# A spectral filter and a low-rank mixer: batch 2's first stage two slots later, and pairs of batches 1 to 3 in other slots

## The chip, the cores and the metric

The kernel runs on one core of a Trainium2 chip. The metric is the time of one execution on the device in microseconds (us). It is taken from runs without a profile; beside them one execution was profiled, and all durations, waits and clocks in this document come from such a profile.

The engines are TensorE (PE in the profile; PEld is its weight load), VectorE (DVE), ScalarE (ACT), GpSimd (POOL) and SyncE (SP). SyncE, ScalarE and GpSimd also issue DMAs. Each engine goes through its own list of instructions in order.

## The reference

```python
def _attn_ref(x, filt_r, filt_i):              # x: 8 x 3136 x 256
    X = np.fft.rfft(x, axis=1)
    Y = X * (filt_r + 1j * filt_i)[None, :, :]
    return np.fft.irfft(Y, n=x.shape[1], axis=1)

def _moe_ref(x, U, V, w_ch1, w_ch2):           # U: 3136 x 32, V: 32 x 3136, w_ch1: 256 x 1024
    h = x.transpose(0, 2, 1) @ U @ V
    u = x + h.transpose(0, 2, 1)
    return u + np.maximum(u @ w_ch1, 0.0) @ w_ch2
```

The second function takes the result of the first. All inputs and the output are float32.

## The kernel before

The Fourier transform of 3136 = 64 x 49 points is done as matmuls in two stages, and so is its inverse. For each batch from 1 to 7 the way is:

- `load_x` (L154) brings one of three chunks of x into a tile `xt`, as float16, by DMAs of GpSimd. There are five such buffers.
- `f1_units` (L451) is the first stage, 13 units for a batch: one matmul (L460) into a PSUM bank `pf` and one eviction into `asb` (L464 on VectorE or L466 on ScalarE). Units 0 to 3 belong to chunk 0, 4 to 7 to chunk 1, 8 to 12 to chunk 2. After a chunk's last unit `asb` is stored into the DRAM scratch `c1` (L470): by SyncE for batch 1, by GpSimd for the others.
- `load_a` (L477) reads `c1` back, rearranged, as one of four tiles `a` of a batch, by SyncE (L480). Each serves four pairs, and there are three buffers.
- `stream` (L526) does the second stage, the filter and the first inverse stage, for 16 pairs of frequencies per batch. A pair is two matmuls into `px` (L499, a single bank) and the product with the filter (for batch 1 `both_products`, L507, one instruction of VectorE; for the others `product`, L518 and L520, three of VectorE, and a sum on GpSimd, L523). The inverse of a pair (`i1`, matmuls L535 into `pi`, eviction L539) is issued `LAG` = 2 pairs later; each fourth one is followed by a store into the scratch `c2` (L542).
- `load_e` (L483) reads `c2` back as the tiles `e2`; `h1_unit` (L563) computes the low-rank part from them.
- The mixer then goes over groups of four row blocks, six groups to a batch: `make_u` (L659), `mm1` (L689, matmuls L694 into `phh`, relu into `h` at L702 or L700) and `mm2` (L704, matmuls L720 or L765 into `po`), with the output behind them.

Batch 0 has a way of its own (`first_f1`, `first_mid`) ahead of the main loop, in which batch 1's first stage begins too. The main loop runs over the mixer's groups of all batches, and everything else of the batches ahead is woven into it by slots: `put(slot, generator)` enters one step in a table, and `run(slot)` issues the steps of a slot in the order in which they were entered. A group has eight slots, a batch `SB` = 48:

```python
        for a in range(4):
            if live:
                mm1(gx, 2 * a)
                mm1(gx, 2 * a + 1)
            if full:
                run(slot)
            ...                       # a == 2: make_u of the next group
            mm2(gx - 1, a)
            if full:
                run(slot + 1)
                slot += 2
            evict(gx - 1, a)
```

The list `steps` holds the slots of the pairs, one entry for each `next` of `stream`. Since this order is written out by hand, an engine's instructions stand in the order of the slots, and a step that must wait holds up all that stands behind it on its engine.

Of the kernel before, what the change touches and what calls it, by code (L numbers as in the profile page):

```python
# [15 lines left out]
NS = 32  # L16
# [5 lines left out]
KG = 8  # L22
LAG = 2
# [66 lines left out]
def kernel(  # L90
# [12 lines left out]
    nb = x.shape[0]  # L103
# [19 lines left out]
    def bank(tag, name):  # L123
        return ps.tile([128, 512], F32, tag=tag, bufs=BUFS[tag], name=name)
# [14 lines left out]
    def natural(ap):  # L139

        return ap.rearrange("p (r i h a) -> p r h i a", i=4, h=2, a=32)

    def split(ap):

        return ap.rearrange("p (r h i a) -> p r h i a", i=4, h=2, a=32)
# [305 lines left out]
    def f1_units(b, both):  # L451
        ne = 0
        for c in range(len(CH)):
            xt = st[b]["x"].pop(c)
            asb = sb.tile([128, 9 * DM], F16, tag="asb", bufs=2, name="asb")
            for n0 in range(0, CH[c], 2):
                w = min(2, CH[c] - n0) * DM
                k = 64 if c0[c] + n0 == NH - 1 else 128
                pf = bank("o" if b == 1 else "m", "pf")
                nc.tensor.matmul(pf[:, 0:w], w64[:, :], xt[:, n0 * DM:n0 * DM + w],  # L460
                                 start=True, stop=True)
                dst = asb[0:k, n0 * DM:n0 * DM + w]
                if both and (ne % 2 if b > 1 else ne > 3 and ne not in (5, 7, 12)):
                    nc.vector.tensor_copy(dst, pf[0:k, 0:w])  # L464
                else:
                    nc.scalar.copy(dst, pf[0:k, 0:w])  # L466
                ne += 1
                if n0 + 2 >= CH[c]:
                    for h, o, n in span(c0[c], c0[c + 1]):
                        (nc.sync if b == 1 else nc.gpsimd).dma_start(c1[b].ap()[:, o:o + n], asb[64 * h:64 * h + 64, 0:n])  # L470
                yield


    def spec(t, gi, p, n):
        return bass.AP(tensor=t, offset=gi * KG * 2 * RD + p * DM, ap=[[DM, n], [2 * RD, KG], [1, DM]])
# [18 lines left out]
    def forward(m, a2, xtags):  # L494
        ml = m % (KG // 2)
        px = bank(xtags[m % len(xtags)], "px")
        for sl in range(2):
            s = 2 * m + sl
            nc.tensor.matmul(px[:, sl * DM:(sl + 1) * DM], t2[:, s * 128:(s + 1) * 128],  # L499
                             a2[:, (2 * ml + sl) * DM:(2 * ml + sl + 1) * DM],  # L500
                             start=True, stop=True, skip_group_check=True)
        return px
# [23 lines left out]
    def stream():  # L526
        pend = []

        def i1(b, m, y, esb):
            pi = bank("f", "pi")  # L530
            nf = 2 if b == 1 else 1
            for sl in range(2):
                for fi in range(nf):
                    g, o = (fi * NS + 2 * m + sl) * 98, fi * 512 + sl * DM
                    nc.tensor.matmul(pi[0:98, sl * DM:(sl + 1) * DM], g12[:, g:g + 98],  # L535
                                     y[:, o:o + DM], start=(fi == 0), stop=(fi == nf - 1),
                                     skip_group_check=True)
            gi, ml = divmod(m, KG // 2)
            nc.scalar.copy(split(esb[:, ml * 512:(ml + 1) * 512]), natural(pi[0:98, :]))  # L539
            if ml == KG // 2 - 1:  # L540
                for p, n in ((0, 96), (96, 2)):
                    (nc.scalar if b == 1 else nc.sync).dma_start(  # L542
                        spec(c2[b], gi, p, n), esb[p:p + n].rearrange("p (k d) -> p k d", d=DM))

        for b in range(1, nb):
            for m in range(NS // 2):
                gi, ml = divmod(m, KG // 2)
                if ml == 0:
                    esb = sb.tile([98, KG * DM], F16, tag="esb", bufs=2, name="esb")
                y = (both_products if b == 1 else product)(m, forward(m, st[b]["a"][gi], ("x",)))  # L550
                if len(pend) == LAG:
                    i1(*pend.pop(0))
                pend.append((b, m, y, esb))
                yield
        for p in pend:
            i1(*p)
            yield

    def one(load, *a):
        load(*a)  # L560
        yield
# [227 lines left out]
    def put(slot, gen):  # L789
        sched.setdefault(int(slot + 0.5), []).append(gen)  # L790
# [6 lines left out]
    NP = NS // 2  # L797
    GP = NP // (NS // KG)
    SB = 48
# [13 lines left out]
    fill = f1_units(1, True)  # L813
# [8 lines left out]
    for k in range(2):  # L822
        put(k, fill)

    steps = [8.8 + 1.25 * k for k in range(NP)] + [28 + 2.45 * k for k in range(NP)]
    for b in range(3, nb):
        steps += [SB * (b - 2) + 18 + 3 * k for k in range(NP)]
    steps += [steps[-1] + 3 * (k + 1) for k in range(LAG)]
    mid = stream()
    for b in range(1, nb):  # L830
        gen = h1_unit(b)
        for t in (8, 7, 6) if b > 1 else (9, 8, 7):
            put(SB * b - t, gen)
    for k, t in enumerate(steps):
        put(t, mid)
        b, m = divmod(k - LAG, NP)
        if k >= LAG and m % GP == GP - 1:
            t += 6 if b > 1 or not b and m < NP - 1 else 4
            late = SB * b + 13
            if b and t < late:  # L840
                put(max(t, SB * b - 1), one(load_e, b + 1, m // GP, (0,)))
                put(late, one(load_e, b + 1, m // GP, (1,)))
            else:
                put(t, one(load_e, b + 1, m // GP))
    for b in range(1, nb):
        for gi in range(NS // KG):
            t = steps[NP * (b - 1) + GP * gi]
            put(max(2, t - (14 if b > 3 else 9 + b // 3)), one(load_a, b, gi))
        if b > 1:
            fill = f1_units(b, b == 2)  # L850
            t0 = steps[NP * (b - 1)]
            for k in range(NF):
                put(4 + 1.1 * k if b == 2 else 18 + 2.8 * k if b == 3 else t0 - 54 + 3 * k, fill)
            for c in range(len(CH)):
                if b > 2 or c > 0:
                    put(6 * c - 5 if b == 2 else 9 + 8 * c if b == 3 else t0 - 72 + 12 * c, one(load_x, b, c))
# [58 lines left out]
```

## Time and profile before

| what | value |
|---|---|
| runs | 533.61, 534.28, 538.67 us; median 534.28 us |
| the profiled execution's own time | 534.16 us |
| its span, first to last instruction | 532.4 us |
| mean granted TensorE clock | 0.988 of full |
| TensorE busy | 498.4 us (94% of the span) |
| VectorE, ScalarE, GpSimd busy | 400.7, 377.7, 290.9 us |
| TensorE idle from 0 to 54.5 us, 54.5 to 160 us, 160 to 500 us | 17.5, 7.2, 3.9 us |

The span is what the rows of the profile cover; the execution's time is 1.8 us longer. The first 54.5 us are batch 0's own way; the main loop's slot 0 is at 54.5 us and slot 66 at 158 us. Waits on engines other than TensorE matter only if TensorE comes to wait for them. A DMA has no busy time on the engine that issues it: its row tells when it was issued. Queue q0 in the DMA counts holds the transfers that GpSimd issues, q1 those of SyncE, q10 those of ScalarE.

### The profile page before, as it was taken

Reading aid. Unit: us, or ns where it says so; the run is one execution under the profiler, and the core shown is the slowest. Engines: PE = TensorE matmul, PEld = TensorE weight load, DVE = VectorE, ACT = ScalarE, POOL = GpSimd, SP = SyncE. Lnnn points to the kernel's source line nnn. Section 1 sums busy time; section 2 is a strip of 40 time slices with the busy share of each in tenths; the row PEclk is TensorE's granted clock in tenths of the full one; section 3 lists DMA queues with packets and bytes.
Section 4 is the critical chain, followed back from the end, with each engine's and each line's share of the span. In section 5 each row is a group of like instructions: output and inputs, shape, how many; then the busy total and the mean of one; then the engine's idle time right before and its main releaser. Section 6 shows DMA issues by size and latency. Waiting matters only on the chain.

```text
span 532.4 us, 11368 instructions
## 1 busy us (share of the span) xinstructions
PE 498.4 (94%) x4022; PEld 303.0 (57%) x4022; DVE 400.7 (75%) x574; ACT 377.7 (71%) x771; POOL 290.9 (55%) x412
## 2 busy tenths in 40 slices
PE   3877799999999999999999999989999999999995
PEld 3765266667667785555555555545555555454444
DVE  7897367757786758898998888978999877445663
ACT  2767756677678868888788878877777678765541
POOL 7797633345656456586677665765756564313000
PEclk9979989999999999999999999999999999999999
DMA  8989998986988577897989798896887575544324
GB/s 127 193 150 188 204 211 210 217 223 147 232 234 214 141 154 221 208 229 171 225 204 220 195 240 205 177 235 145 199 194 148 126 180 128 140 96 80 78 66 104
DMA packets 118426, 93.98 MB, mean 177 GB/s; under 512 B 52977, under 2 KB 100786, under 8 KB 118370
## 3 DMA queue, kind: packets, MB, share of 16 engines
q0 software_dynamic: 21936, 41.91, 38.3%
q1 hardware_dynamic: 93226, 49.75, 37.7%
q10 hardware_dynamic: 3208, 1.61, 1.1%
q8 instruction: 31, 0.51, 0.4%
q14 instruction: 25, 0.20, 0.1%
HBM read 56.25 MB, written 48.17 MB: 196 GB/s over the span
## 4 chain that ended last, share of the span: by engine, by line
PE 79%; DVE 6%; POOL 6%; DMA 6%; issue 2%; ACT 1%; DVEq 0%; POOLq 0%; ACTq 0%
PE phh L694 27%; PE po L765 21%; PE po L720 8%; PE px L499 5%; PE pi L535 5%; PE pu L620 4%; DVE uv L520 3%; PE pf L460 3%; DMA xt<-in_x_dram 3%; PE ph L577 2%; POOL low L284 2%; DVE uv L518 1%; DMA vq<-in_moe_V_dram 1%; DMA g<-gd 1%; POOL xt L154 1%
## 5 line engine op out<-in xcount | busy, mean ns | idle before, releaser
L702 ACT ACTIVATE h<-phh 128x512 f16<-128x512 f32 (+1 forms) x391 | 205.9, 578 | 71.8 <-PE phh L694 66.9
L694 PE MATMUL phh<-ut,w 128*128 128x512 f16 x768 | 197.6, 379 | 0.6 <-ACT h L702 0.3
L523 POOL TENSOR_TENSOR y<-uv 128x512 f16<-128x512 f16 x96 | 111.0, 1158 | 110.6 <-DVE uv L520 74.8
L765 PE MATMUL po<-h,w 128*128 128x512 f16 x560 | 143.8, 379 | 0.0
L520 DVE TENSOR_TENSOR uv<-px,ft 64x512 f16<-64x512 f32 x192 | 132.1, 688 | 2.6
L694 PEld LDWEIGHTS <-w 128*128 128x128 f16 x832 | 78.5, 98 | 77.2 <-issue 2.4
L518 DVE TENSOR_TENSOR uv<-px,ft 128x512 f16<-128x512 f32 x96 | 65.3, 680 | 42.1 <-PE px L499 35.8
L783 POOL DMA_DIRECT2D out_dram<-och x120 | 70.2, 592 | 42.9 <-DVE och L775 35.6
L539 ACT CAST esb<-pi 98x512 f16<-98x512 f32 x112 | 66.0, 589 | 36.9 <-PE pi L535 33.9
L765 PEld LDWEIGHTS <-w 128*128 128x128 f16 x560 | 51.6, 98 | 53.2 <-issue 1.1
L774 DVE TENSOR_TENSOR tt<-po,ut 128x512 f32<-128x512 f32 x70 | 48.4, 692 | 33.8 <-PE po L765 30.9
L720 PE MATMUL po<-w,h 128*128 128x256 f16 x448 | 58.9, 275 | 0.0
L499 PE MATMUL px<-a,t 98*128 98x256 f16 x256 | 50.0, 277 | 7.2 <-DVE uv L520 3.7
L775 DVE STREAM_TRANSPOSE och<-tt 128x512 f32<-128x512 f32 x70 | 49.8, 711 | 2.4
L466 ACT CAST asb<-pf 128x512 f16<-128x512 f32 (+1 forms) x79 | 45.7, 578 | 5.3 <-PE pf L460 4.2
L720 PEld LDWEIGHTS <-h 128*128 128x128 f16 x448 | 42.8, 98 | 10.8 <-issue 1.4
L507 DVE TENSOR_TENSOR uv<-px,ft 128x1024 f16<-128x1024 f32 x32 | 38.0, 1219 | 13.9 <-PE px L499 13.4
L499 PEld LDWEIGHTS <-t 98*128 98x128 f16 x256 | 23.0, 99 | 33.9 <-DVE uv L520 11.5
L535 PE MATMUL pi<-y,g 128*98 128x256 f16 x192 | 36.7, 271 | 2.0 <-POOL y L523 2.0
L684 ACT CAST ut<-pu 128x512 f16<-128x512 f32 x70 | 38.1, 610 | 0.0
L460 PE MATMUL pf<-xt,w 128*128 128x512 f16 (+1 forms) x91 | 33.4, 373 | 3.3 <-DMA xt<-in_x_dram 3.0
L535 PEld LDWEIGHTS <-g 128*98 128x98 f16 x256 | 29.6, 123 | 4.0 <-issue 2.1
(96 smaller groups left out, 445.0 us busy)
## 6 DMA issues: line engine op xcount, KB each, us to landing
xt<-in_x_dram POOLq DMA_DIRECT2D x46, 256.0 KB, 6.7
a<-c SPq DMA_DIRECT2D x28, 384.0 KB
e<-c SPq DMA_DIRECT2D x56, 192.0 KB
out_dram<-och SPq DMA_DIRECT2D x160, 64.0 KB
c<-esb SPq DMA_DIRECT2D x24, 384.0 KB
c<-asb POOLq DMA_DIRECT2D x30, 256.0 KB, 4.9
out_dram<-och POOLq DMA_DIRECT2D x120, 64.0 KB, 3.2
out_dram<-och POOLq DMA_DIRECT2D x24, 256.0 KB, 4.9
```

Of the source, the lines that this page charges most:

```text
L499: nc.tensor.matmul(px[:, sl * DM:(sl + 1) * DM], t2[:, s * 128:(s + 1) * 128], a2[:, (2 * ml + sl) * DM:(2 * ml + sl + 1) * DM], start=Tru ...
L518: nc.vector.tensor_mul(uv[:, 0:512], px[:, :], ft[:, a:a + 512])
L520: nc.vector.tensor_mul(uv[p:p + 64, 512:1024], px[q:q + 64, :], ft[q:q + 64, b:b + 512])
L523: nc.gpsimd.tensor_add(y, uv[:, 0:512], uv[:, 512:1024])
L535: nc.tensor.matmul(pi[0:98, sl * DM:(sl + 1) * DM], g12[:, g:g + 98], y[:, o:o + DM], start=(fi == 0), stop=(fi == nf - 1), skip_group_che ...
L539: nc.scalar.copy(split(esb[:, ml * 512:(ml + 1) * 512]), natural(pi[0:98, :]))
L694: nc.tensor.matmul(pm[:, 0:w], w1[:, dh * 1024 + t * 128:dh * 1024 + (t + 1) * 128], ut[:, dh * w:(dh + 1) * w], start=(dh == 0), stop=(dh ...
L702: nc.scalar.activation(h[:, 0:w], pm[:, 0:w], RELU)
L720: nc.tensor.matmul(po[:, o:o + DM], hs[gx, t][:, rr * 128:(rr + 1) * 128], w2[:, t * DM:(t + 1) * DM], start=(t == 0), stop=False, skip_gr ...
L765: nc.tensor.matmul(po[:, :], w2[:, t * DM + dh * 128:t * DM + (dh + 1) * 128], hs[gx, t][:, :], start=(t == 0), stop=(t == 7))
L775: nc.vector.transpose(och.rearrange("p (j h a) -> p h j a", h=2, a=32)[:, dh], tt.rearrange("p (j t) -> p j t", t=32))
L783: (nc.gpsimd if k and b < nb - 1 else nc.sync).dma_start(dst, och[32 * i:32 * i + 32, k * 512:(k + 1) * 512] .rearrange("p (r e) -> p r e" ...
```

## The change

- Batch 2's 13 first-stage units go from slots 4 + 1.1k to 6 + 1.2k (rounded: 4 to 17 before, 6 to 20 after). The loads of x keep their slots: batch 2's chunks 1 and 2 in slots 1 and 7, batch 3's chunks 0, 1 and 2 in slots 9, 17 and 25.
- Batch 1's last two inverses were issued with batch 2's first two pairs (slots 28 and 30); they get steps of their own (slots 29 and 30). Batch 7's last two had such steps already, and keep them.
- Batch 2's pairs go from 28 + 2.45k to 30 + 2.35k (last one in slot 65 in both), batch 3's from 66 + 3k to 67.5 + 2.9k (last one in slot 111 in both). Batch 1's pairs and those of batches 4 to 7 keep their slots.
- `load_a` and `load_e` follow their pairs by the new helper `pair(b, m)`: batch 2's four `load_a` go from slots 19, 29, 39, 48 to 22, 31, 41, 50, batch 3's first two from 56 and 68 to 58 and 69. `load_e` calls are entered after the pairs, so that within a slot they come after a pair and its inverse and no longer before.

```diff
@@ stream
-        for p in pend:
-            i1(*p)
-            yield
+            while pend and b in (1, nb - 1):
+                i1(*pend.pop(0))
+                yield
@@
-    steps = [8.8 + 1.25 * k for k in range(NP)] + [28 + 2.45 * k for k in range(NP)]
-    for b in range(3, nb):
+    steps = [8.8 + 1.25 * k for k in range(NP + LAG)] + [30 + 2.35 * k for k in range(NP)]
+    steps += [SB + 19.5 + 2.9 * k for k in range(NP)]
+    for b in range(4, nb):
         steps += [SB * (b - 2) + 18 + 3 * k for k in range(NP)]
@@
-    for k, t in enumerate(steps):
+    for t in steps:
         put(t, mid)
-        b, m = divmod(k - LAG, NP)
-        if k >= LAG and m % GP == GP - 1:
-            t += 6 if b > 1 or not b and m < NP - 1 else 4
-            late = SB * b + 13
-            ...
+
+    def pair(b, m):
+        return NP * (b - 1) + m + (LAG if b > 1 else 0)
+
     for b in range(1, nb):
         for gi in range(NS // KG):
-            t = steps[NP * (b - 1) + GP * gi]
-            put(max(2, t - (14 if b > 3 else 9 + b // 3)), one(load_a, b, gi))
+            t = steps[pair(b, GP * gi + GP - 1) + LAG]
+            t += 6 if b > 2 or b == 1 and gi < 3 else 4
+            late = SB * (b - 1) + 13
+            if b > 1 and t < late:
+                put(max(t, SB * (b - 1) - 1), one(load_e, b, gi, (0,)))
+                put(late, one(load_e, b, gi, (1,)))
+            else:
+                put(t, one(load_e, b, gi))
+    for b in range(1, nb):
+        for gi in range(NS // KG):
+            t = steps[pair(b, GP * gi)]
+            put(max(2, t - (14 if b > 3 else (9, 8, 10)[b - 1])), one(load_a, b, gi))
         if b > 1:
             fill = f1_units(b, b == 2)
-            t0 = steps[NP * (b - 1)]
+            t0 = steps[pair(b, 0)]
             for k in range(NF):
-                put(4 + 1.1 * k if b == 2 else 18 + 2.8 * k if b == 3 else t0 - 54 + 3 * k, fill)
+                put(6 + 1.2 * k if b == 2 else 18 + 2.8 * k if b == 3 else t0 - 54 + 3 * k, fill)
             for c in range(len(CH)):
                 if b > 2 or c > 0:
                     put(6 * c - 5 if b == 2 else 9 + 8 * c if b == 3 else t0 - 72 + 12 * c, one(load_x, b, c))
```

More of the change, by code (lines that the diff above doesn't have):

```diff
@@ L833 @@
             put(SB * b - t, gen)
-    for k, t in enumerate(steps):
+    for t in steps:
         put(t, mid)
-        b, m = divmod(k - LAG, NP)
-        if k >= LAG and m % GP == GP - 1:
-            t += 6 if b > 1 or not b and m < NP - 1 else 4
-            late = SB * b + 13
[L840 to L844, printed above, removed]
+    def pair(b, m):
+        return NP * (b - 1) + m + (LAG if b > 1 else 0)
     for b in range(1, nb):
         for gi in range(NS // KG):
-            t = steps[NP * (b - 1) + GP * gi]
-            put(max(2, t - (14 if b > 3 else 9 + b // 3)), one(load_a, b, gi))
+            t = steps[pair(b, GP * gi + GP - 1) + LAG]
[10 more added lines that the diff above has]
+            put(max(2, t - (14 if b > 3 else (9, 8, 10)[b - 1])), one(load_a, b, gi))
         if b > 1:
             fill = f1_units(b, b == 2)
-            t0 = steps[NP * (b - 1)]
+            t0 = steps[pair(b, 0)]
             for k in range(NF):
-                put(4 + 1.1 * k if b == 2 else 18 + 2.8 * k if b == 3 else t0 - 54 + 3 * k, fill)
+                put(6 + 1.2 * k if b == 2 else 18 + 2.8 * k if b == 3 else t0 - 54 + 3 * k, fill)
             for c in range(len(CH)):
```

## The prediction

> **What bounds the kernel now.** I read the page first, then TensorE's waits, the timelines around the slots that the change touches, and the DMA counts of a few stretches.
>
> ```profile
> PE 498.4 (94%) x4022; PEld 303.0 (57%) x4022; DVE 400.7 (75%) x574; ACT 377.7 (71%) x771; POOL 290.9 (55%) x412
> ```
>
> TensorE is busy for 498.4 of 532.4 us. Of its 34 idle us 17.5 lie before the main loop starts at 54.5 us, 7.2 between there and 160 us, where the changed slots are, and 3.9 from 160 to 500. So in the loop a wait of TensorE that goes, or comes, moves the end by about its own length. Its waits that lie in the changed slots, from its timeline (start, length, then the idle time before it and who ended that):
>
> ```profile
> 59.53 0.38 PE L460 MATMUL pf<-xt,w 128*128 128x512 f16 x1 [1.15 <-DMA xt<-in_x_dram]
> 66.15 0.58 PE L460 MATMUL pf<-xt,w 128*128 128x512 f16 x1 [1.85 <-DMA xt<-in_x_dram]
> 66.53 1.91 PE L720 MATMUL po<-w,h 128*128 128x256 f16 x8
> 68.45 0.63 PE L499 MATMUL px<-a,t 98*128 98x256 f16 x2
> 70.83 1.03 PE L720 MATMUL po<-w,h 128*128 128x256 f16 x8
> 104.00 0.38 PE L499 MATMUL px<-a,t 98*128 98x256 f16 x2 [0.99 <-DVE uv L507]
> 145.84 0.39 PE L499 MATMUL px<-a,t 98*128 98x256 f16 x2 [0.55 <-DVE uv L520]
> 158.11 0.39 PE L499 MATMUL px<-a,t 98*128 98x256 f16 x2 [1.18 <-DVE uv L520]
> ```
>
> The first two are first-stage units 0 and 4 of batch 2 (slots 4 and 8), waiting for x. 68.45 is batch 1's first pair (slot 9): it did not wait. 104.00 is batch 2's first pair, in one slot with batch 1's last; 158.11 is batch 3's first, one slot behind batch 2's last. The eight po matmuls took 1.91 us at 66.53 and 1.03 at 70.83: the clock. The windows (length, PE busy with instruction count, then the other engines, PEclk, DMA share, GB/s) say so:
>
> ```profile
> 62.49:65.90 3.41, 1.51 (x8) 0.48 (x5) 0.69 (x1) 2.38 (x6) 1.66 (x3) 1.00 0.98 203
> 65.90:69.32 3.42, 3.17 (x15) 1.98 (x16) 0.20 (x1) 0.59 (x1) 3.34 (x8) 0.50 1.20 217
> 69.32:72.73 3.41, 3.03 (x23) 2.13 (x22) 2.94 (x4) 1.08 (x2) 0.33 (x1) 1.00 1.10 286
> ```
>
> In this trace the granted clock changes only at edges 3.41 us apart: a stretch with 1.51 us of work is followed by one at 0.50, and a full one restores 1.00.
>
> **What the slots do to the queues.** GpSimd's and SyncE's own rows:
>
> ```profile
> 58.12 1.18 POOL L154 DMA_DIRECT2D xt<-in_x_dram x2
> 64.24 1.09 POOL L470 DMA_DIRECT2D c<-asb  x2 [4.94 <-ACT ul L296]
> 65.31 1.24 POOL L154 DMA_DIRECT2D xt<-in_x_dram  x2
> 67.91 1.17 POOL L154 DMA_DIRECT2D xt<-in_x_dram  x2
> ...
> 61.83 4.95 SPq L480 DMA_DIRECT2D a<-c  x6
> ```
>
> GpSimd issues x chunk 1 of batch 2 at 58.12, then stands for 4.94 us at the store of batch 2's first stage (unit 3, slot 7), and only behind it come x chunk 2 (65.31, slot 7) and batch 3's chunk 0 (67.91, slot 9). Unit 3 moves to slot 10, but these two loads stay in slots 7 and 9. So they pass the store: both buffers are free (batch 1's units ended at 56.15, the copies out of vq before 56.2), and GpSimd issues them at about 59.3 to 61.4 and, after one copy of 0.55, 62.0 to 63.1. That is the loss that I expect: SyncE issues batch 1's a tiles at 61.83, as soon as its c1 stores have landed (trace: 61.55), and these move beside the x loads. Packets by queue, in four stretches (66 to 69, 64 to 66, 149.5 to 151.5, 62 to 64 us, in this order):
>
> ```profile
> q1 hardware_dynamic: 1277, 0.64, 118.4%
> ...
> q1 hardware_dynamic: 751, 0.38, 73.9%
> q0 software_dynamic: 57, 0.09, 26.5%
> ...
> q0 software_dynamic: 213, 0.59, 94.8%
> q1 hardware_dynamic: 102, 0.05, 9.5%
> ...
> q0 software_dynamic: 162, 0.29, 91.0%
> ```
>
> Alone, the a loads on q1 move 1277 packets of 512 B in 3 us, 426 per us. Beside a full q0 (149.5 to 151.5, the end of a later a tile) they get 51 per us, fewer than q0's 107. I read this as taking turns packet by packet, with packets of q0 four times the size.
>
> **The sum, part by part.**
>
> 1. Units 0 and 4 no longer wait for x. TensorE comes to slot 9 at 68.45 less 3.00 of waits, less two units that now lie behind it (two pf, some 0.22 apart: 0.43) and less about 0.8 of half clock: 64.2 us.
>
> 2. There it waits for the a tile, which landed at 67.89 in the trace. After: from 64.0 q0 still holds 57 packets of chunk 1 and, at 2 KB, 272 and 256 of the two loads (512 + 32 and 512 KB): some 585, 37 for each of 16 engines. A q0 packet costs an engine 0.142 us (71 to 76 us: 607 packets at 107.6% of 16 engines over 5 us) to 0.180 (the row of 62 to 64), a q1 packet 0.0445. Turn by turn 37 x (0.187 to 0.225) = 6.9 to 8.3 us. By then 585 of the tile's 768 packets are through, and the rest takes 0.4: it lands at 71.3 to 72.7, I take 72.0. Bounds: 67.9, if the x loads cost it nothing (at 64 to 66 q1 had 751 packets beside 57); 74.7, if it ends only after a share like the trace's, where some 1550 a packets had moved by 67.89 since the engines are uneven: (1550 - 585) / 426 = 2.3 behind 72.3. I take turns by packet, since the stretch at 150 us is nearest to a q0 that stays full. The first pair starts at 72.1 instead of 68.45: **+3.65**, and the two units behind it **+0.43**. Everything of TensorE is queued behind that pair; ACT and VectorE starve with it, and GpSimd then stands at the store of slot 10.
>
> 3. Clock. The stretch 65.90 to 69.32 would hold no work, 69.32 to 72.73 0.6 us, so 0.50 stays until the next edge, 76.14. Half clock costs half of its time (1.91 against 1.03 above): 0.5 x (76.14 - 72.1) = 2.0, against 0.5 x 0.87 = 0.43 behind 68.45 now: **+1.6**. Bounds: -0.4 (no drop) to +2.0.
>
> The Trainium skill ("TensorE: Matmul & The Clock Gate", "What's actually happening") has the half rate come after an idle window of about 3.4 us. Here 1.51 us of work in 3.41 was followed by 0.50, so the measurement decides against a need for a wholly idle one. Both give half clock for a wait to 72; for a shorter wait they differ, see the rivals.
>
> 4. Batch 1's last inverses get slots 29 and 30, batch 2's pairs start in slot 30, batch 3's in 68 instead of 66. The px bank has one buffer, so two pairs in one slot or in neighbours wait for the product: **-0.99** (104.00) and **-1.18** (158.11). A wait of 0.28 of a unit for an eviction at 84.02 I count **-0.2**. The matmuls stay the same in number.
>
> 5. New near neighbours: pairs in slots 54, 56, 58 repeat today's 53, 55, 57, whose waits (0.19, and 0.55 at 145.84) stay; 30/32 and 61/63/65 are new: 0.19 + 0.19 + 0.55 = **+0.9**. Slots 37/39 and 44/46 are as near, but the low-rank sums and a make_u lie between them; without that cover 0.55 each. So +0 to +2.0.
>
> 6. At nothing: load_a(2,0) goes from slot 19 to 22 and its store from 17 to 20, behind x chunk 1 of batch 3 (slot 17) on GpSimd's queue. Slot 20 was at 88.6, after at 94.2; store issued at 95 and landed by 100.5 (now 4.7 us, and some time behind x), tile 4.7 us later (89.99 to 94.72 now) at 105.2; it is read in slot 30 at 108.0 + 5.7 - 1.0 = 112.7. Its cover is 7.5 us; past it each us costs one. SyncE waits meanwhile with load_e(1,1) behind it, read from slot 39 on; load_e(1,0) now stands ahead of it. load_a(2,3) and load_e(2,0) shift with their pairs (138.67 against a reader at 145.84). The other load_e calls only change places within a slot.
>
> Sum: 3.65 + 0.43 + 1.6 - 0.99 - 1.18 - 0.2 + 0.9 = +4.2. The profiled execution's own time is 534.16 us (span 532.4), the median of the runs 534.28: 534.16 + 4.2 = **538.4**.
>
> **Rivals.** (a) The x loads don't hold up the tile: it lands at 67.9, TensorE waits from 64.2 to 68.0 and the clock is at 0.50 until 72.73. -0.45 + 0.43 + (2.37 - 0.43) - 1.5 = +0.4: 534.6. For it: 751 beside 57. Against: the 102 beside 213. In this case the change does not do what it says in slots 4 to 9: one wait takes the other's place.
>
> (b) The other side: as (a), but the clock holds through this wait. It decides at how much work the stretch 62.49 to 65.90 (1.7 us, then idle) and the next one (1.3 us) must hold. -0.45 + 0.43 - 0.43 - 1.5 = -1.9: 532.2. Against it stand 1.51 above, and 1.60 before the drop at 28.36. The rule of the skill named in step 3 leads here, as no whole window is idle.
>
> (c) Without any wait in slot 9: -4.25 + 0.43 - 0.43 - 1.5 = -5.7: 528.4. The tile would have to land at 64.3, 2.5 us after its issue; the fastest a loads here took 4.6.
>
> (d) More starving: the tile lands at 74.7, half clock until 79.55: 6.25 + 0.43 + 2.0 - 0.5 = +8.2: 542.4. It decides at whether the engines that finish x last also hold the tile's last rows, as in the trace.
>
> **Chances.** Forecast 0.50 (its own range 536.3 to 540.6), (a) 0.20, (b) 0.10, (c) 0.03, (d) 0.17. The range 531.6 to 542.0 leaves out (c) and over half of (d). One per cent, about what a measurement of this kernel can tell from no change, is 5.3 us: over 539.6 are (d) and 0.10 of the forecast, so 0.27; under 529.0 is (c), 0.03; within 0.70.
>
> **What would show it.** Right: no wait for xt at 59 and 66 us; x loads issued on GpSimd without the stop of 4.94; a wait of 6 to 9 us of px on the a tile near 64 to 72; granted clock 0.50 behind it; no wait at batch 2's and 3's first pairs. Wrong: px starts before 69 (step 2), the clock back at 1.00 before it resumes (step 3), waits above 0.6 us at pairs of batch 2 (step 5), or a wait of batch 2's first pair for its tile (step 6).

## The result, and the profile after

The changed kernel is slower: median 548.54 us (547.20 to 550.38, 6 runs) against 533.63 us (530.93 to 538.67, 6 runs), a ratio of 1.0279 with a 95% interval of 1.0228 to 1.0330. That is 14.9 us where +4.2 was forecast. Its profiled execution took 550.38 us (span 548.6) against 534.16 (532.4): 16.2 more. A few executions took over 1.5% longer than the fastest of their kernel; the ratios and medians below are without them, and no line below is from a profile of one.

TensorE has the same 4022 instructions on the page, and is busy for 6 us more and idle for 10 us more. The 6 us are nearly all half clock: from 54 to 500 us, 15.0 us of its busy time lie at half clock, against 3.2 before.

```profile
PE 504.7 (92%) x4022; PEld 305.4 (56%) x4022; DVE 401.2 (73%) x574; ACT 378.8 (69%) x771; POOL 291.6 (53%) x412
```

TensorE's waits of the changed kernel from 54 to 160 us (who, for whom: us in total, times, longest):

```profile
PE px L499 <- DMA a<-c: 13.1, 2, 7.9
...
PE px L499 <- DVE uv L520: 0.5, 2, 0.3
```

The waits for x and the 0.99 us at batch 2's first pair are gone, as the change meant. In their place px waits twice for a tile `a`, 13.1 us. From TensorE's timeline:

```profile
63.85 1.04 PE L720 MATMUL po<-w,h 128*128 128x256 f16 x8
64.72 0.28 PE L724 MATMUL po<-idn,ut 128*128 128x128 f16 x2
72.95 0.61 PE L499 MATMUL px<-a,t 98*128 98x256 f16 x2 [7.95 <-DMA a<-c]
...
147.69 0.58 PE L499 MATMUL px<-a,t 98*128 98x256 f16 x2 [5.20 <-DMA a<-c]
...
219.79 0.39 PE L499 MATMUL px<-a,t 98*128 98x256 f16 x2 [1.18 <-DVE uv L520]
```

72.95 is batch 1's first pair (slot 9; 68.45 before, without a wait). 147.69 is batch 2's ninth, the first reader of its third tile, (2, 2). 219.79 is batch 3's twelfth pair (0.08 us before). In the kernel before, batch 2's ninth did not wait:

```profile
133.56 0.38 PE L499 MATMUL px<-a,t 98*128 98x256 f16 x2
```

The clock drops during both long waits and stays low behind them (length, then busy times, PEclk, DMA share, GB/s). The first two rows lie ahead of every changed step:

```profile
51.27:54.68 3.41, 2.08 (x15) 0.95 (x14) 2.13 (x4) 0.96 (x3) 3.41 (x6) 1.00 1.14 225
54.68:58.09 3.41, 3.41 (x10) 1.37 (x9) 1.04 (x2) 2.50 (x5) 2.60 (x5) 0.50 0.87 167
...
64.92:68.33 3.41, 0.08 (x2) 0.00 (x0) 0.00 (x0) 0.04 (x1) 0.00 (x0) 1.00 1.13 213
68.33:71.75 3.42, 0.00 (x0) 0.00 (x0) 0.00 (x0) 0.00 (x0) 0.00 (x0) 0.50 1.12 236
71.75:75.16 3.41, 2.21 (x7) 1.00 (x8) 1.23 (x1) 0.60 (x1) 0.00 (x0) 0.50 1.03 185
75.16:78.57 3.41, 3.41 (x18) 2.45 (x17) 1.89 (x3) 0.60 (x1) 0.45 (x1) 0.50 0.03 6
78.57:81.98 3.41, 3.41 (x25) 1.91 (x24) 2.95 (x4) 2.60 (x5) 1.20 (x3) 1.00 0.63 154
...
143.43:146.84 3.41, 0.00 (x0) 0.00 (x0) 0.00 (x0) 0.00 (x0) 0.39 (x1) 1.00 1.07 248
146.84:150.25 3.41, 2.56 (x9) 1.33 (x10) 1.85 (x3) 1.25 (x3) 0.00 (x0) 0.50 0.48 176
150.25:153.67 3.42, 3.42 (x17) 2.33 (x16) 0.61 (x2) 1.05 (x3) 1.15 (x1) 0.50 0.72 162
```

Where the 16.2 us arise is seen from the matmuls of `mm1`, the same in both kernels. The 17th (slot 8) starts 0.5 us earlier than before, the 25th (behind the first pair) 6.1 later, the 97th (ahead of the second wait) 7.8, the 113th (behind the second wait) 15.1, the 241st (behind 219.79) 16.2, the last 16.2. So there are two steps of 6.6 and 7.3 us, a small one of 1.1, and 1.7 us that gather between the two large ones, from work that now comes later in the order and from smaller waits (0.84 us for an eviction at 90.86, 0.41 for a tile `e` at 127.23), less the 0.99 that is gone. Some 0.7 of the 16.2 us is not the change's: this execution's main loop began 1.0 us sooner than that of the kernel before, and the stretch at half clock from 54.68 to 58.09 cost it 1.7.

The first step is the forecast one. GpSimd issues the x loads without a stop and stands behind them:

```profile
58.27 2.36 POOL L154 DMA_DIRECT2D xt<-in_x_dram  x4
...
62.00 1.18 POOL L154 DMA_DIRECT2D xt<-in_x_dram  x2
78.12 1.09 POOL L470 DMA_DIRECT2D c<-asb  x2 [14.94 <-issue]
```

Packets of the two queues from 66 to 70 us:

```profile
q0 software_dynamic: 420, 0.66, 88.7%
q1 hardware_dynamic: 406, 0.21, 24.4%
```

One for one: 406 packets of a in 4 us, where 1277 went in 3 us before. By the trace 96 of the first tile's 98 rows had landed at 72.64 us and the last two at 72.90, and TensorE went on at 72.95.

The second step is on SyncE's queue (first what it waited for from 112 to 152 us, then its rows):

```profile
SPq L594 <- DVE e L588: 9.8, 1, 9.8
...
133.38 1.38 SPq L594 DMA_DIRECT2D e<-e  x2
...
135.45 2.16 SPq L599 DMA_DIRECT2D e<-e  x1
137.71 2.54 SPq L480 DMA_DIRECT2D a<-c  x2
140.35 1.99 SPq L542 DMA_DIRECT2D c<-esb  x2
149.82 0.58 SPq L487 DMA_DIRECT2D e<-c  x1
150.45 1.02 SPq L480 DMA_DIRECT2D a<-c  x2
```

The a load at 137.71 is tile (2, 2). In the kernel before it was issued in slot 39, at 116.14, and the store into `c2` went out ahead of the copies as well:

```profile
116.14 0.96 SPq L480 DMA_DIRECT2D a<-c  x2
124.96 1.87 SPq L542 DMA_DIRECT2D c<-esb  x2
126.93 2.53 SPq L594 DMA_DIRECT2D e<-e  x2
```

In slot 41 the load comes behind the third step of `h1_unit(1)`, whose four copies into `e2` (L594 to L599) wait for VectorE until 133.4. Batch 4's first x load had been issued just before it, and the tile landed only at 147.5:

```profile
136.76 1.25 POOL L154 DMA_DIRECT2D xt<-in_x_dram  x2
...
139.81 7.74 DMA a<-c
```

The last row is from the chain of work that ended last: the landing ends at 147.55. The a load at 150.45 is the fourth tile, (2, 3), behind `load_e(2, 0, (0,))` at 149.82, which stood for the store into c2 issued at 140.35.

### The profile page after: what moved, and what is told of

It reads as the page before. It is cut to its first block, busy times and chain, and to the rows that moved or that the text cites. A ratio compares the mean times of both kernels' runs of the same rounds, so it can differ in the third digit from the quotient of the medians.

```text
span 548.6 us, 11361 instructions
## 1 busy us (share of the span) xinstructions
PE 504.7 (92%) x4022; PEld 305.4 (56%) x4022; DVE 401.2 (73%) x574; ACT 378.8 (69%) x771; POOL 291.6 (53%) x412
## 4 chain that ended last, share of the span: by engine, by line
PE 75%; DMA 9%; DVE 8%; POOL 3%; issue 2%; ACT 1%; SPq 1%; ACTq 0%; DVEq 0%; POOLq 0%
PE phh L694 27%; PE po L765 21%; PE po L720 7%; PE px L499 5%; PE pi L535 5%; PE pu L620 4%; DMA a<-c 3%; DVE uv L520 3%; PE pf L460 3%; PE ph L577 2%; DVE uv L518 2%; DMA c<-asb 1%; DMA ft<-in_filt_r_dram 1%; DMA g<-gd 1%; DVE uv L507 1%
## 5 line engine op out<-in xcount | busy, mean ns | idle before, releaser
L694 PE MATMUL phh<-ut,w 128*128 128x512 f16 x768 | 200.5, 384 | 1.8 <-DVE asb L464 0.8
L499 PE MATMUL px<-a,t 98*128 98x256 f16 x256 | 51.0, 282 | 19.1 <-DMA a<-c 13.1
L470 POOL DMA_DIRECT2D c<-asb x36 | 19.6, 549 | 32.8 <-issue 22.2
```

Source lines behind the costliest of these rows:

```text
L694: nc.tensor.matmul(pm[:, 0:w], w1[:, dh * 1024 + t * 128:dh * 1024 + (t + 1) * 128], ut[:, dh * w:(dh + 1) * w], start=(dh == 0), stop=(dh ...
```

## The experiments

Ratios are to the kernel before, run beside it on the same chip, with 95% intervals; 0.01 is 5.3 us. Most intervals reach some 2 us to either side, so the difference of two ratios is known to some 3 us. "Changed" is the changed kernel (1.0279).

### The first stall: x loads and the store

**x loads behind the store again (e1_x_behind).**

```diff
-put(6 * c - 5 if b == 2 else 9 + 8 * c if b == 3 else ..., one(load_x, b, c))
+put((0, 1, 10)[c] if b == 2 else (11, 17, 25)[c] if b == 3 else ..., one(load_x, b, c))
```

> The changed kernel, with the load of x chunk 2 of batch 2 in slot 10 instead of 7 and that of batch 3's chunk 0 in slot 11 instead of 9, so that both stand behind the store of unit 3 on GpSimd's queue again. Theory A (the x loads that passed the store hold up batch 1's first a tile): the tile lands near 68 us instead of 72.8, the wait of px for it falls from 7.9 to about 3.5 us, the 5.2 us wait near 147 stays: 4 to 6 us less than the changed kernel's 548.5, so 543 to 544.5. Rival (the tile is late for another reason, or the wait is only that TensorE comes early): wait of 7 us or more and 547 to 549.

Measured: 1.0193 [1.0146, 1.0240], 4.6 us under changed. Theory A holds in its size, as far as three executions tell it. Most of the rest of this stall stays, as expected: without the x loads' part the wait is still 4 us (shown below in a profile with the same order of loads).

**x loads ahead, in the kernel before (e6_x_ahead_only).** The same line with `(0, 1, 6)[c]` and `(6, 17, 25)[c]`; nothing else of the change.

> The kernel before with one thing alone: the x loads of slots 7 and 9 (batch 2's chunk 2, batch 3's chunk 0) in slot 6, ahead of the store of unit 3. Units, pairs and a loads stay. Theory A: GpSimd issues them near 59 to 62 us, the first a tile lands near 72.5 instead of 67.9, px waits 4 to 5 us for it and the clock drops behind it: 538 to 541. Rival (the loads cost nothing, the wait came from TensorE's earlier arrival alone): 533 to 534.5.

Measured: 1.0171 [1.0122, 1.0220], +9.1 us, more than expected. TensorE's timeline:

```profile
77.20 0.58 PE L499 MATMUL px<-a,t 98*128 98x256 f16 x2 [8.33 <-DMA a<-c]
```

The order of GpSimd's loads alone makes a stall of 8.33 us, with the units in their old slots. The rival falls. The profile is of the slowest of the four executions, and not all of its time is this stall: a wait of 2.28 us ahead of the main loop and half clock from 55.02 to 61.84 us are part of it. In it the store into `c1`, for which the a load must wait, was slow beside the x loads too (6.08 us, from 60.03 to 66.11).

**The units back (e5_units_back).**

```diff
-put(6 + 1.2 * k if b == 2 else ..., fill)
+put(4 + 1.1 * k if b == 2 else ..., fill)
```

> The changed kernel with one part undone: batch 2's first-stage units at 4 + 1.1k again, pairs and loads as changed. Theory A: the store of unit 3 is again ahead of the x loads, the wait of px for the first a tile goes, the waits of 1.15 and 1.85 us for x come back, and the wait near 147 stays: 541 to 543, that is 6 us under the changed kernel and 8 over the one before. If the units' move had paid by the waits that it took away, this kernel would be slower than the changed one: 550 or more.

Measured: 1.0137 [1.0092, 1.0181], 540.17 us, 7.6 us under changed. The waits for x are back (1.25 and 1.07 us in its profile), px waits 0.3 us for batch 1's first tile, and the wait at batch 2's third tile stays at 5.0 us. The units' move, with the x loads that pass the store by it, cost much more than the waits that it took away.

### The second stall: SyncE's queue

**The third tile ahead of h1_unit's step (e2_a22_first).**

```diff
+    put(41, one(load_a, 2, 2))          # entered before the loop over h1_unit
     for b in range(1, nb):
         gen = h1_unit(b)
         ...
```

The same call is left out of the loop over `load_a` further down.

> The changed kernel, with batch 2's third a tile still loaded in slot 41, but entered ahead of h1_unit's third step in that slot, so that its two DMAs stand on SyncE's queue ahead of the four copies into e2 (L594 to L599) and not behind them. Theory B (the tile is late since SyncE stands at those copies): the load is issued near 124 us instead of 137.7, the 5.2 us wait of px at 147.7 and most of the 6.8 us at half clock there go, 8 us less: 540 to 541.5. Rival (pairs of batch 2 too close, or the x load of batch 4 beside it): the tile is still waited for, over 546.

Measured: 1.0220 [1.0179, 1.0261], 545.36 us: 3 us under changed, not 8, and hardly clear of noise. In the profile (543.27 us) the mechanism is as expected:

```profile
122.60 1.02 SPq L480 DMA_DIRECT2D a<-c  x2
...
149.01 1.02 SPq L480 DMA_DIRECT2D a<-c  x2
```

The third tile is issued at 122.60, and no px waits for a tile of batch 2. But the fourth (149.01) has a reader at 155.84, 6.8 us later; the third had needed 9.8 us in the changed kernel. The median lies 2 us above this one profile, and what the other executions waited for is not in it; the next experiment asks for it.

**Third and fourth tile (e14_both_tiles).** As before it, and `put(46, one(load_a, 2, 3))` beside the added line.

> The changed kernel with batch 2's third a tile ahead of h1_unit's third step (slot 41) and its fourth in slot 46; units and x loads as changed, so that only theory A's stall is left. Theory C (where the third tile alone was mended, the fourth was late in its place and took back part of the gain): no px waits for an a tile of batch 2, 540 to 542, that is 3 to 4 us less than with the third tile alone. Rival (the fourth tile plays no part there, and the third is worth only 3 us): 544 to 546.

Measured: 1.0121 [1.0088, 1.0154], 540.17 us, as expected. Both tiles together are worth 8.4 us, of which the fourth gives 5; this interval and that of the third tile alone do not meet. That the fourth is late in executions with the third tile alone mended is inferred from these times; in a profile it is seen in the kernel with the pairs' part alone, below.

**The third tile behind h1_unit's step, in the kernel before (e7_a22_late_only).**

```diff
-put(max(2, t - (14 if b > 3 else 9 + b // 3)), one(load_a, b, gi))
+put(41 if (b, gi) == (2, 2) else max(2, t - (14 if b > 3 else 9 + b // 3)), one(load_a, b, gi))
```

> The kernel before with one thing alone: batch 2's third a tile loaded in slot 41 behind h1_unit's third step instead of in slot 39 ahead of it. Theory B: it is issued near 131 us instead of 116, beside the x load of 127.5, lands at 137.5 to 139, and the pair that reads it at 133.6 waits 4 to 5 us, half clock behind it 2 us: 538.5 to 541. Rival (the wait in the changed kernel comes from the closer pairs): under 1 us, 533 to 534.5.

Measured: 1.0216 [1.0173, 1.0259], +11.5 us. Theory B holds, and is worth more alone than in the changed kernel:

```profile
131.10 2.21 SPq L480 DMA_DIRECT2D a<-c  x2
...
142.17 0.58 PE L499 MATMUL px<-a,t 98*128 98x256 f16 x2 [8.57 <-DMA a<-c]
```

Issued at 131.10 as expected, but landed near 142, not at 139; the wait is 8.57 us. Closer pairs are not in this kernel, so they are not needed for it.

**Batch 4's x load later (e4_x40_late).** The load of (4, 0) in slot 48 instead of 42, the rest as changed.

> The changed kernel, with batch 4's first x load in slot 48 instead of 42, everything else as changed. It tells the two parts of the late third a tile apart: issued late (137.7 us, needed at 142.5) and slow (9.9 us to land instead of 4.6 without an x load beside it). If late issue alone decides, the tile still comes 4 us late or more: 547 to 548.5. If the x load beside it is needed too, it lands near 142.5, the wait falls to under 1 us and the half clock goes: 540 to 542.

Measured: 1.0170 [1.0131, 1.0209], 542.30 us.

```profile
137.83 2.68 SPq L480 DMA_DIRECT2D a<-c  x2
...
144.41 0.38 PE L499 MATMUL px<-a,t 98*128 98x256 f16 x2 [1.79 <-DMA a<-c]
```

The tile is issued as late as in the changed kernel, but the wait for it is 1.79 us instead of 5.20, and the clock stays at full there. Late issue alone is not enough: the x load beside it makes up two thirds of the wait. The expected wait of under 1 us was missed, and the time by a little.

### Both, and what is left

**x loads behind, third tile ahead (e3_both).** The edits of e1_x_behind and e2_a22_first.

> Both of the two edits: x loads behind the store (slots 10 and 11) and the third a tile ahead of h1_unit's third step. Theories A and B together: 5 and 8 us, so 534.5 to 537, near the kernel before and not below it, since a wait of 3 to 4 us at batch 1's first pair has taken the place of the two waits for x. If the two stalls are one chain (the first makes the second), the sum is less than that of the single edits: 539 or more.

Measured: 1.0077 [1.0035, 1.0118], 538.37 us, just under the bound given for one chain of stalls, and above the sum. Its profile has a wait of 1.95 us at 151.82 for the fourth tile: one more stall, uncovered by mending the others.

**The pairs' part alone (e8_pairs_only).** Units at 4 + 1.1k, third tile ahead.

> The part of the change that moves pairs and inverses alone: the changed kernel with the units at 4 + 1.1k again and the third a tile ahead of h1_unit's third step. What is left is batch 1's last inverses in slots of their own, batch 2's pairs from 30 and batch 3's from 67.5. By the waits of the profile before: 0.99 and 1.18 us go, 0.9 us at close pairs of batch 2 and 1.1 us at two close pairs of batch 3 (seen at 219.8 us in the changed kernel) come: within 1 us of the kernel before, 533 to 534.5. If A and B are not the whole of the loss: 537 or more.

Measured: 1.0065 [1.0012, 1.0117], 537.53 us, so A and B, as far as these two edits undo them, are not the whole:

```profile
131.00 2.62 SPq L542 DMA_DIRECT2D c<-esb  x2
143.17 0.58 SPq L487 DMA_DIRECT2D e<-c  x1
143.79 1.09 SPq L480 DMA_DIRECT2D a<-c  x2
...
149.64 0.38 PE L499 MATMUL px<-a,t 98*128 98x256 f16 x2 [2.41 <-DMA a<-c]
```

`load_e(2, 0, (0,))` stands 9.5 us until the store of 131.00 has landed, and the fourth tile behind it is issued at 143.79. Before, that store went out at 124.96, ahead of the copies into `e2`; now inverse 3 of batch 2 is in slot 42, behind them.

**Fourth tile in slot 46 as well (e10_a23_too).** Added: `put(46, one(load_a, 2, 3))`.

> As the kernel with the pairs' part alone (units at 4 + 1.1k, third a tile ahead of h1_unit's third step), and batch 2's fourth a tile loaded in slot 46 instead of 50, ahead of load_e(2,0), which stands on SyncE's queue from 133.6 to 143.2 us there until a store into c2 has landed. Theory C (that stop makes the fourth tile late: a wait of 2.4 us at 149.6 and one stretch of 3.4 us at half clock): 4 us less than 537.5, so 533 to 534.5. Rival (the rest of the loss is spread over the closer pairs): 536.5 or more.

Measured: 1.0028 [0.9988, 1.0069]. In its profile (533.68 us) no px waits for a tile. So the wait that theory C names is gone. In time, the step from 1.0065 to 1.0028 is within the noise; that the fourth tile costs time is shown by the kernel with both tiles mended. The difference to the kernel before is within its interval.

**Batch 3's twelfth pair in slot 100 (e11_spread3).**

```diff
-    steps += [SB + 19.5 + 2.9 * k for k in range(NP)]
+    steps += [68, 70, 73, 76, 79, 82, 85, 88, 91, 94, 97, 100, 102, 105, 108, 111]
```

> As the one with the fourth tile in slot 46, and batch 3's twelfth pair in slot 100 instead of 99, so that the two pairs that are two slots apart have a make_u between them. Theory D (1.17 us of px at 208.8 come from these two pairs' nearness and an output copy on VectorE between them): 1 us less, 532 to 533.5, which is the gain that the moved pairs were worth, 0.99 and 1.18 less what the closer pairs of batch 2 cost. Rival (the wait only moves to the next pair): the same as without it, 533 to 534.5.

Measured: 1.0025 [0.9995, 1.0055], no gain. The wait of 1.18 us became one of 0.31 at that pair and one of 0.71 at the next, which comes two slots later: the rival's case. Theory D falls as a way to a gain.

**The units late, all else mended (e12_units_late_rest).** The x loads of e1_x_behind, the tiles of e14_both_tiles.

> The changed kernel with its three late tiles mended: x loads behind the store (slots 10 and 11), third a tile ahead of h1_unit's third step, fourth in slot 46; the first-stage units stay two slots later. Beside the kernel with the units at 4 + 1.1k it tells what the units' move is worth by itself. By the profiles: 3.0 us of waits for x go, a wait of 4.3 us for the first a tile with half clock behind it comes: 1.5 to 2.5 us slower than that kernel, 535 to 537. If the move pays once nothing is in its way: under 533.

Measured: 1.0073 [1.0031, 1.0115], as expected slower than e10_a23_too (medians 537.38 and 533.96 us, side by side on one chip). The units' move, with nothing in its way, turns the waits for x into

```profile
67.54 0.61 PE L499 MATMUL px<-a,t 98*128 98x256 f16 x2 [4.21 <-DMA a<-c]
```

TensorE comes sooner to a tile that is not there yet.

**Batch 4's x load in slot 48 too (e13_x40_too).** As e11_spread3, with the edit of e4_x40_late.

> As the one with batch 3's twelfth pair in slot 100, and batch 4's first x load in slot 48 instead of 42, out of the way of the stores into c2 and the a tiles of batch 2. If that load still costs TensorE something there: 1 us less or more than that, 531 to 532.5. If all tiles are in time anyway: the same time, 532 to 533.5.

Measured: 1.0014 [0.9970, 1.0058]: no difference that can be told from e11_spread3. No version beat the kernel before.

From 1.0279 down, one edit at a time: third tile 1.0220, fourth 1.0121, x loads behind the store 1.0073, units back 1.0028. The last of these edits puts the x loads back into their slots too, still behind the store. So some 3.1, 5.3, 2.6 and 2.4 us, and 1.5 us that can't be told from nothing; 3.1, 2.6 and 2.4 are each within the noise of such a difference, though the medians of the last two kernels, side by side, bear out the last one. The shares depend on the order in which the parts are mended, as the larger effects of the x loads and the third tile alone (9.1 and 11.5 us) show.

## Why the prediction was right and wrong

**Steps 1 and 2 were right.** TensorE came to slot 9 at 65.0 (64.2 said), the tile's 96 rows landed at 72.64 and its last two at 72.90 (72.0), px waited 7.95 us (7.9). That the wait agrees so closely is luck, as both of its ends came 0.8 to 0.9 us later than said. TensorE came late by about the 0.7 us that this execution lost ahead of slot 4. That the two queues take turns packet by packet was a choice, as 102 beside 213 is not one for one; the 420 beside 406 bear it out. Rivals (a) to (c), with the tile at 68 or sooner, are out, and so is (d), with the tile at 74.7.

**Step 3 was right in kind and small by 0.8 us.** The edges lay elsewhere in this execution (64.92, 68.33, ... against 65.90, 69.32), so half clock lasted 5.6 us behind the first pair and not 4.0: 2.8 against 2.0. The stretches with 2.21 and 2.56 us of work at half clock did not restore it, the ones filled did. The rule of the Trainium skill ("TensorE: Matmul & The Clock Gate", "What's actually happening") agrees for the drops at 68.33 and 146.84, as the stretches ahead of them held 0.08 and 0.00 us of work. The drop at 54.68 came behind a stretch with 2.08 us of work, which is no idle one; there, as in step 3, the measurement decides.

**Step 4 was right**: no wait at the first pairs of batches 2 and 3. The wait of 0.28 for an eviction at 84.02 went, but another eviction held `mm1` up for 0.84 at 90.86.

**Step 5** said +0.9 at batch 2's near pairs. Its pairs waited 0.34, 0.15, 0.19, 0.26 and 0.19 us, 1.1 in all, where 0.74 of that kind had been counted: +0.4. What it left out is batch 3, where 2.9 instead of 3 puts two pairs in slots 97 and 99: +1.1.

**Step 6 failed, and with it the forecast.** It put the moved loads at nothing. Its sentence that load_a(2,3) and load_e(2,0) "shift with their pairs" priced a move in slots, and load_a(2,2) it did not name at all. Two slots later, the third tile and the store behind inverse 3 both fell behind the four copies of `h1_unit`'s third step in slot 41, which wait for VectorE. So the third tile went out 21.6 us later (137.71 against 116.14), not two slots later. Its cover had been 13.1 us (landed at 120.44, reader at 133.56), and its reader now came 8.9 us later. But it landed among batch 4's x packets and took 9.8 us for that, not 4.3: the same starving as in step 2, at a place that the prediction did not price. Together that leaves TensorE some 5 us short, the wait of 5.20. The fourth tile's row was misread as well. Of the sixteen landings that the trace has for its 96 rows, 138.67 is the first and 141.99 the last, so its cover ahead of the reader at 145.84 was not 7 us but 3.9; in the kernel with the pairs' part alone the stop of load_e for the store (9.5 us) took it. In place of "at nothing" stand 8.4 us (1.0279 to 1.0121).

With 8.4 for step 6, 0.8 more for step 3 and +1.5 in place of +0.9 for step 5, the sum would have been +14.0, where 14.9 was measured; the rest is within the interval. It is a rough sum, as the 8.4 depends on the order of the edits.

Three slips of the working change nothing in this. 72.3 and 2.3 are 74.6, not 74.7. Rival (d) takes steps 4 and 5 at -0.5, where the others have -1.5, and shows no row for it. And the fastest a load of the trace took 3.45 us (381.13 to 384.58), not 4.6, which is still too long for rival (c).

What would prove step 6 wrong was also named too narrowly: a late first tile of batch 2, which did not come; the third and fourth did.

## What to carry to other kernels

When steps move in a schedule that is written out by hand, list the order of every queue before and after, not the slots: a load that passes one instruction which waits is not late by its slots but by that wait. An idle-looking DMA load that is moved ahead can starve the small packets of the load that is needed next, as the x loads did here (406 packets of a in 4 us, where 1277 had gone in 3). And a wait that is taken away early pays only if what comes behind it is ready sooner too.

## What was not expected of the hardware

The issue of a load by SyncE took very different times. Right behind the copies into `e2`, two a loads took 2.54 us to issue at 137.71, and 2.30 at 131.69 before, against 0.96 at 116.14, away from them; the last of the copies (L599) took 2.16 against 0.81. It is not these copies alone: in the changed kernel two a loads behind a `load_e` took 2.18 us at 119.49, and one DMA of batch 1's a loads 4.33 at 63.17. What the slow ones have in common was not tested.

The edges of the clock's stretches keep their 3.41 us, but lie at other places of the program in each execution: a 4.2 us wait cost one such stretch at half clock in e12_units_late_rest (67.58 to 70.99), a 7.95 us wait three in the changed kernel.
